# Decay and causal fill added by VectorE from rows spread over all partitions, and attention's order planned with seeds

## Chip, core and metric

One core of a Trainium2 chip runs the whole program in one launch. The metric is device time in microseconds of that core, the median of three runs. A profile of one further execution gives the trace.

## What is computed

Attention with a decay, then two feed-forward layers, all in float32. The core of it:

```python
q, k, v: (4, 8, 576, 64), f: (4, 8, 576)
scores = scale * np.matmul(q, k.transpose(0, 1, 3, 2))
cum = np.cumsum(np.log(np.clip(f, 0.0001, 1.0)), axis=-1)
decay = cum[:, :, :, None] - cum[:, :, None, :]
scores = np.where(causal, -1000000000.0, scores + decay)
scores = scores - np.max(scores, axis=-1, keepdims=True)
attn = np.exp(scores)
attn = attn / (np.sum(attn, axis=-1, keepdims=True) + 1e-09)
x = (attn @ v) as (2304 tokens, 512)
h = x @ w_in;  x = (h / (1 + np.exp(-h))) @ w_out      # 2048 hidden
out = ((x @ w_a) * (x @ w_b)) @ w_out2                 # 1536 hidden
```

## The kernel before

*Attention.* The 32 heads go through in 16 pairs; the two heads of a pair lie on partitions 0 to 63 and 64 to 127 of one tile. A head's 576 query rows are five blocks (`IB`): four of 128 rows and one of 64. Block 0 meets 128 key columns, block 1 256, block 2 384, block 3 512; the two 64-row blocks of a pair share one pass over 576 columns, in two halves of 288. `score` (L519 on) makes the scores of a pair in the groups (4,), (3,), (2,), (1, 0), each in two of the four PSUM banks of tag `s`. A float32 product is made of three products in float32r: q and k are split into hi and lo (`load_parts`, L501: ScalarE or VectorE casts hi, GpSimd subtracts for lo in four pieces, L516), and hi·hi, hi·lo and lo·hi are summed in PSUM. In pairs 1 to 15 a fourth product comes first: the tile `dt` in bfloat16 holds, per head, six rows with the cumulative sum split in three bfloat16 parts and constants, so that this product gives the decay (L564, step 0). These rows are made in `prepare` (L437 to L449) and go through the DRAM tensor `dec`. Pair 0 (`QK32`) is made in whole float32 instead, with two extra rows for the decay (L558); its rows of the sum are loaded straight from `cum` (L489).

*After the scores.* VectorE reads a block from PSUM, adds the causal mask tile `maskw` or `mask2`, scales by -1/8 and takes the row minimum in one instruction (L590, `tensor_tensor_reduce`); the first half of the 64-row blocks needs no mask and has `tensor_scalar` (L586). ScalarE takes the exponential and the row sum (L598). TensorE turns the probabilities (L640), ScalarE or VectorE copies them out of PSUM (L645, L646), TensorE multiplies with v (L684), VectorE divides by the row sums, which come spread over partitions through DRAM (L613 to L621, L693), and ScalarE and GpSimd split the result into hi and lo of `x`.

*Feed-forward.* Weights come as float64 words and are decoded to float32 hi and lo (`plan_decode`, `decode`), in 13 chunks of hidden units. Chunk 0 and the decoding of chunks 0, 1 and 2 are planned together with attention; the products of chunk 0 (L766 to L768) are the filler work there. Chunk 1's tiles lie in a pool of their own and are decoded (`decode1`) while attention runs. From chunk 1 on (L311 to L313) the order is written by hand.

*Order.* Up to the end of chunk 0 the order of all engines comes from `Plan.order` (L171): a list scheduler that has a price for each operation (`t_mm`, `t_dve`, `t_act`, `t_pool`, and for DMAs the bytes divided by 230), a priority, and tags that count buffers; it takes the operation that can start first, and among those within 30 ns the one of the lowest priority value. Each engine runs its operations in the order that comes out. `keep_warm` puts small idle products (L805) where the plan sees TensorE idle early on; `run_up` puts 66 of them at the start.

## Time and profile before

| | |
|---|---|
| median of 3 runs | 1037.66 us (1037.36 to 1039.34) |
| the profiled execution: time, span | 1037.98 us, 1036.1 us |
| TensorE (PE) busy | 1020.9 us, 99% of the span |
| weight loads (PEld) | 846.7 us, 82% |
| VectorE (DVE) | 656.1 us, 63% |
| ScalarE (ACT) | 444.5 us, 43% |
| GpSimd (POOL) | 334.5 us, 32% |
| moved by DMA | 62.35 MB, mean 60 GB/s |

Busy time of an engine is the union of its instructions. Products on TensorE overlap: one may start 0.2 us after another and both last 0.4 us, so what a product costs is the distance to the next start. The row of a line and tile names what is written and read: `s<-decay` is a score bank written from the decay tile. A wait is put down to the engine whose semaphore came last.

### The profile page before, as it was taken

Reading aid. Unit: us, or ns where it says so; the run is one execution under the profiler, and the core shown is the slowest. Engines: PE = TensorE matmul, PEld = TensorE weight load, DVE = VectorE, ACT = ScalarE, POOL = GpSimd, SP = SyncE. Lnnn points to the kernel's source line nnn. Section 1 sums busy time; section 2 is a strip of 40 time slices with the busy share of each in tenths; the row PEclk is TensorE's granted clock in tenths of the full one; section 3 lists DMA queues with packets and bytes.
Section 4 is the critical chain, followed back from the end, with each engine's and each line's share of the span. In section 5 each row is a group of like instructions: output and inputs, shape, how many; then the busy total and the mean of one; then the engine's idle time right before and its main releaser. Section 6 shows DMA issues by size and latency. Waiting matters only on the chain.

```text
span 1036.1 us, 16198 instructions
## 1 busy us (share of the span) xinstructions
PE 1020.9 (99%) x5813; PEld 846.7 (82%) x5813; DVE 656.1 (63%) x1539; ACT 444.5 (43%) x1080; POOL 334.5 (32%) x414
## 2 busy tenths in 40 slices
PE   8989999999999999999999999999999999999998
PEld 7667777798888888888888788888888888888887
DVE  7885566648976856857648976166375485473334
ACT  7888888855433324323324445332132231231111
POOL 5574444434412503304006853051150150240000
PEclk9999999999999999999999999999999999999999
DMA  5443333212210201201101222021021030020012
GB/s 165 151 135 111 101 100 105 63 63 71 72 52 21 81 23 31 82 11 44 39 1 41 61 60 83 1 72 52 1 82 41 2 95 27 21 61 1 10 72 102
DMA packets 34096, 62.35 MB, mean 60 GB/s; under 512 B 7004, under 2 KB 8684, under 8 KB 33984
## 3 DMA queue, kind: packets, MB, share of 16 engines
q1 hardware_dynamic: 33904, 60.87, 19.0%
q8 instruction: 46, 0.75, 0.3%
q10 hardware_dynamic: 112, 0.45, 0.2%
q14 instruction: 34, 0.28, 0.1%
HBM read 56.05 MB, written 5.23 MB: 59 GB/s over the span
## 4 chain that ended last, share of the span: by engine, by line
PE 83%; DVE 5%; ACT 2%; issue 1%; DMA 1%; POOL 1%; POOLq 0%; ACTq 0%; DVEq 0%; SPq 0%
PE ps L311 14%; PE ps L313 14%; PE ps L312 14%; PE po L312 10%; PE po L313 9%; PE po L311 9%; PE s L564 3%; PE pv L684 3%; PE t_y L640 1%; PE t_x L640 1%; DVE acc L365 1%; DMA d<-in_w 1%; DVE d L277 1%; PE po L766 1%; PE ps L766 1%
## 5 line engine op out<-in xcount | busy, mean ns | idle before, releaser
L311 PE MATMUL ps<-x,whi 128*128 128x512 f32 (+1 forms) x760 | 279.9, 368 | 0.4 <-DVE acc L365 0.4
L312 PE MATMUL ps<-x,whi 128*128 128x512 f32 (+1 forms) x760 | 279.7, 368 | 0.0
L313 PE MATMUL ps<-x,wlo 128*128 128x512 f32 (+1 forms) x760 | 279.6, 368 | 0.0
L281 POOL TENSOR_TENSOR d<-d,whi 128x256 f32<-128x256 f32 x116 | 98.2, 850 | 420.8 <-ACT whi L280 379.0
L312 PE MATMUL po<-glo,whi 128*128 128x512 f32 (+1 forms) x520 | 191.4, 368 | 0.6 <-DVE glo L344 0.6
L313 PE MATMUL po<-ghi,wlo 128*128 128x512 f32 (+1 forms) x520 | 191.1, 368 | 0.0
L311 PE MATMUL po<-ghi,whi 128*128 128x512 f32 (+1 forms) x520 | 189.7, 369 | 0.6 <-ACT ghi L343 0.6
L311 PEld LDWEIGHTS ps<-x,whi 128*128 128x128 f32 x760 | 143.3, 189 | 24.8 <-issue 0.8
L313 PEld LDWEIGHTS ps<-x,wlo 128*128 128x128 f32 x760 | 143.3, 189 | 23.9
L312 PEld LDWEIGHTS ps<-x,whi 128*128 128x128 f32 x760 | 143.3, 189 | 23.7
L343 ACT CAST ghi<-g 128x512 fp32r<-128x512 f32 (+1 forms) x130 | 74.8, 576 | 141.6 <-DVE g L342 94.6
L311 PEld LDWEIGHTS po<-ghi,whi 128*128 128x128 f32 x520 | 97.9, 189 | 17.7 <-ACT ghi L343 1.4
L312 PEld LDWEIGHTS po<-glo,whi 128*128 128x128 f32 x520 | 98.1, 189 | 17.2 <-DVE glo L344 0.9
L344 DVE TENSOR_TENSOR glo<-g,ghi 128x512 fp32r<-128x512 f32 (+1 forms) x130 | 89.1, 686 | 35.7 <-ACT ghi L343 35.3
L313 PEld LDWEIGHTS po<-ghi,wlo 128*128 128x128 f32 x520 | 98.0, 188 | 16.3
L342 DVE TENSOR_TENSOR g<-g,ps 128x512 f32<-128x512 f32 (+1 forms) x60 | 37.9, 631 | 115.4 <-PE ps L313 114.8
L282 POOL TENSOR_TENSOR wlo<-d,d 128x256 fp32r<-128x256 f32 x116 | 91.2, 790 | 36.1 <-DVE d L279 32.8
L273 ACT ACTIVATE d<-d 128x256 f32<-128x256 f32 x116 | 50.5, 435 | 121.0 <-DMA d<-in_w 98.9
L365 DVE SCALAR_TENSOR_TENSOR acc<-po,acc 128x512 f32<-128x512 f32 (+3 forms) x144 | 76.2, 549 | 24.9 <-PE po L313 24.7
L274 DVE TENSOR_SCALAR d<-d 128x256 uint32<-128x256 uint32 x116 | 44.6, 384 | 63.5 <-ACT d L273 62.7
L374 DVE TENSOR_TENSOR acc<-po,acc 128x512 f32<-128x512 f32 (+2 forms) x120 | 64.5, 553 | 25.6 <-PE po L313 25.0
L341 ACT COPY g<-ps 128x512 f32<-128x512 f32 (+1 forms) x60 | 32.4, 540 | 103.8 <-PE ps L313 103.8
(129 smaller groups left out, 1486.7 us busy)
## 6 DMA issues: line engine op xcount, KB each, us to landing
d<-in_w SPq DMA_DIRECT2D x124, 256.0 KB
qk<-in_qk SPq DMA_DIRECT2D x15, 608.0 KB
vt<-in_v SPq DMA_DIRECT2D x16, 320.0 KB
rb<-invs SPq DMA_DIRECT2D x32, 128.0 KB
out_t<-acc SPq DMA_DIRECT2D x12, 256.0 KB
d2ghi<-in_w SPq DMA_DIRECT2D x8, 256.0 KB
e<-in_w SPq DMA_DIRECT2D x4, 256.0 KB
out_t<-acc SPq DMA_DIRECT2D x4, 192.0 KB
```

The costliest lines, as they stand in the source:

```text
L273: nc.scalar.activation(m, high.bitcast(F32), AF.Copy, scale=2.0 ** -112)
L274: nc.vector.tensor_scalar(m.bitcast(U32), m.bitcast(U32), 3, None, ALU.logical_shift_left)
L281: nc.gpsimd.tensor_sub(m, val, hi.bitcast(F32))
L282: nc.gpsimd.tensor_add(lo, m, e)
L311: nc.tensor.matmul(ps, wh, mh, start=start, stop=False)
L312: nc.tensor.matmul(ps, wh, ml, start=False, stop=False)
L313: nc.tensor.matmul(ps, wl, mh, start=False, stop=stop)
L342: nc.vector.tensor_mul(g, g, project(c, 1, t, t0, n)[:, :n])
L343: nc.scalar.copy(ghi[:, t, :n], g)
L344: nc.vector.tensor_sub(glo[:, t, :n], g, ghi[:, t, :n].bitcast(F32))
L365: nc.vector.scalar_tensor_tensor(a, ps, 0.5, a, ALU.mult, ALU.add)
L374: nc.vector.tensor_add(a, ps, a)
```

## The change

- The bfloat16 decay product of pairs 1 to 15 goes, with its tile `dt`. A row's own decay term is constant along the row and drops out of the softmax, so only the negated sum of the key columns, `cn` = -8 cum, remains to be added. It is stored once as `dec` (32 x 576 float32), and each pair loads it with every partition reading the same row: `ws` (64 partitions per head, 576 columns, for the 64-row blocks) and `wd[p]` (128 partitions, 512 columns, one per head).
- VectorE's `tensor_tensor_reduce` adds `ws` or `wd[p]` where it added the mask. `tensor_scalar` remains in pair 0 alone.
- The causal fill is put into these tiles by GpSimd: `hide` writes MASKED above the diagonal of 128 columns of `wd[p]`, first those of block 3; once VectorE has read block 3, those of block 2, and so on. For `ws` the 64-column mask is added once.
- Pair 0 takes q and k from the packed tile, both heads in halves of the array, and gets its `cn` row by an fp32 product with a selection matrix `sel` (`pick`, L572 of the new kernel).
- Chunk 1's weight tiles take the slots of `qkh` and its decoding those of `wd` and `p`, so it follows the last pair (`plan_early`).
- `shake` adds random amounts, by 60 fixed seeds, to the priorities of some operations. Prices change: DMA bytes by 330 in place of 230, ScalarE 2% and GpSimd 10% dearer, VectorE's decode steps half as dear again. `RUN_UP` is 30 in place of 66.

```diff
+SHAKES = (
+    98418, 636944, 799308, 878264, 960778, 981929, 617613, 565829, 424101, 929226, 581331, 653776,
...
+def shake(ops, seed):
+
+    rng = Random(seed)
+    n, by = rng.choice((1, 2, 4, 8, 30, len(ops) // 4)), rng.choice((0.3, 1.0, 3.0))
+    for op in rng.sample(ops, n):
+        op.prio += rng.gauss(0, by)
...
-        self.add("DMA", size / 230, lambda: None, reads, writes, 0, 950)
+        self.add("DMA", size / 330, lambda: None, reads, writes, 0, 950)
...
-    return base + n / 1.2
+    return 1.02 * (base + n / 1.2)
 
 
 def t_pool(n):
-    return 133 + 2.135 * n
+    return 146 + 2.35 * n
...
-    dec = dram.tile([NH, 6, 2, S], BF16, name="dec")
+    dec = dram.tile([NH, S], F32, name="dec")
...
-    rows_sb = dp.tile([NH, 6, 2, S], BF16, name="rows")
+    cn = dp.tile([NH, S], F32, name="cn")
+    maskw = dp.tile([P, 512], F32, name="maskw")
+    sel = dp.tile([NH, 3, P], F32, name="sel")
...
-    RUN_UP, WARM = 66, 40000
-    rows_keys = [("rows", n) for n in range(2)]
+    RUN_UP, WARM = 30, 40000
...
+        plan.add("DVE", 300, lambda: nc.vector.tensor_scalar(cn, cum, -1 / SCALE, None, ALU.mult), ["cum"], [("rows", "cn")], -8)
+        plan.dma(480, 74000, lambda: nc.scalar.dma_start(dec, cn), [("rows", "cn")], ["dec"], pr, eng="ACT")
+        plan.add("POOL", 200, lambda: nc.gpsimd.memset(sel, 1.0), (), [("rows", "sel")], -9.8)
+        for n, base, steps, op in ((0, 0, 0, ALU.is_equal), (1, -1, 0, ALU.is_equal)):
+            plan.add("POOL", 244, lambda n=n, base=base, op=op: nc.gpsimd.affine_select(
+                sel[:, n], sel[:, n], pattern=[[0, P]], compare_op=op, fill=0.0, base=base, channel_multiplier=1),
+                (), [("rows", "sel")], -9.8)
...
-        for n in range(3):
-            src = cum if n == 0 else rest[n - 1]
-            plan.add("DVE", 450, lambda n=n, src=src: nc.vector.tensor_copy(rows_sb[:, n, 0], src), [("c", n), "cum"], [("rows", n)], -8)
-            if n < 2:
-                plan.add("DVE", 750, lambda n=n, src=src: nc.vector.tensor_sub(rest[n], src, rows_sb[:, n, 0]),
-                         [("c", n), ("rows", n), "cum"], [("c", n + 1), ("f", "one")[n]], -8)
-        for n in range(3):
-            plan.add("ACT", 530, lambda n=n: nc.scalar.copy(rows_sb[:, 3 + n, 1], rows_sb[:, n, 0]), [("rows", n)], [("rows", "k", n)], -8)
...
+    def hide(wd, n, pr):
+        plan.add("POOL", 300, lambda: nc.gpsimd.affine_select(
+            wd()[:, n * P:(n + 1) * P], wd()[:, n * P:(n + 1) * P], pattern=[[-1, P]], compare_op=ALU.is_ge,
+            fill=MASKED, base=0, channel_multiplier=1), (), [(wd, n)], pr + PRIO["max"])
...
+        wd = [buf(sb, "wd", [P, 512], F32, f"wd_{pair}_{p}") for p in range(2)]
+        ws = buf(sb, "ws", [P, S], F32, f"ws_{pair}")
...
+        def wide(h, rows, n):
+            src = dec[h]
+            return bass.AP(tensor=src.tensor, offset=src.offset, ap=[[0, rows], [1, n]])
+
         for p in range(2):
-            plan.dma(400, 0, lambda p=p: nc.sync.dma_start(
-                dt()[p * D:p * D + 6, :2 * S], dec[2 * pair + p].rearrange("r i t -> r (i t)")), ["dec", ("decay", n)], [(dt, p)], pr)
-            plan.dma(400, 0, lambda p=p: nc.sync.dma_start(
-                dt()[p * D:p * D + 6, 2 * S + p * D:2 * S + (p + 1) * D], dec[2 * pair + p, :, 0, 512:]), ["dec", ("decay", n)], [(dt, 2 + p)], pr)
+            plan.dma(480, 4 * D * S, lambda p=p: nc.sync.dma_start(ws()[p * D:(p + 1) * D], wide(2 * pair + p, D, S)),
+                     ["dec"], [(ws, p)], pr)
+        plan.add("POOL", 270, lambda: nc.gpsimd.tensor_add(ws()[:, -D:], ws()[:, -D:], mask2[:, -D:]),
+                 [(ws, 0), (ws, 1), ("const", 3)], [(ws, "m")], pr)
+        for p in range(2):
+            plan.dma(480, 4 * P * 512, lambda p=p: nc.sync.dma_start(wd[p](), wide(2 * pair + p, P, 512)),
+                     ["dec"], [(wd[p], n) for n in range(4)], pr)
+            hide(wd[p], 3, pr)
...
-                    a, b = ((t["dt"],) * 2, (t["hi"], t["hi"]), (t["hi"], t["lo"]), (t["lo"], t["hi"]))[step]
+                    out = banks[part]()[:, :nj] if shared else banks[p]()[:, at:at + nj]
+                    a, b = (t["s1"],) * 2 if whole else ((t["hi"], t["hi"]), (t["hi"], t["lo"]), (t["lo"], t["hi"]))[step]
                     a, b = (half(x(), p) if p is not None else x() for x in (a, b))
-                    k0, q2 = (2 * S - S, 2 * S) if step == 0 else (512, Q2)
-                    stat = a[:, i] if p is not None else a[:, q2:q2 + P]
-                    nc.tensor.matmul(out, stat, b[:, k0 + j0:k0 + j0 + nj], start=step == 0, stop=step == 3)
...
+            if whole:
+
+                def pick(at=at, nj=nj):
+                    for n in range(2):
+                        out, j0 = (banks[n]()[:, :nj], n * nj) if shared else (banks[n]()[:, at:at + nj], 0)
+                        nc.tensor.matmul(out, sel[:, 2 if shared else n], cn[:, j0:j0 + nj], start=False, stop=True)
+
+                plan.add("PE", 2 * (nj / 0.6 + 20), pick, [("rows", "cn"), ("rows", "sel")], banks, pr + PRIO["s"], mode=PICK)
...
+            t = heads[2 * pair]
+            if whole:
+                add, keys = (lambda p=p, nj=nj: (mask2 if p is None else maskw)[:, -nj:]), [("const", 3) if p is None else ("rows", "mask")]
+            elif shared:
+                add, keys = (lambda t=t, j0=j0, nj=nj: t["ws"]()[:, j0:j0 + nj]), [(t["ws"], n) for n in (0, 1, "m")]
             else:
-                mk = mask2[:, -nj:] if p is None else maskw[:, -nj:]
-                plan.add("DVE", t_dve(nj) + 82, lambda out=out, low=low, o=o, mk=mk: nc.vector.tensor_tensor_reduce(
-                    out(), o(), mk, -SCALE, 3.0e38, ALU.add, ALU.min, low()), [s, ("const", 3)], [(b, j0), (nm, col)], pr + PRIO["max"])
+                add, keys = (lambda t=t, p=p, nj=nj: t["wd"][p]()[:, :nj]), [(t["wd"][p], n) for n in range(ib + 1)]
+            plan.add("DVE", t_dve(nj) + 82, lambda out=out, low=low, o=o, add=add: nc.vector.tensor_tensor_reduce(
+                out(), o(), add(), -SCALE, 3.0e38, ALU.add, ALU.min, low()), [s, *keys], [(b, j0), (nm, col)], pr + PRIO["max"])
+            if not whole and not shared and ib:
+                hide(t["wd"][p], ib - 1, pr)
...
-        plan.add("DVE", t_dve(n, True), lambda: nc.vector.tensor_scalar(u(m), u(m), 3, None, ALU.logical_shift_left),
+        plan.add("DVE", 1.5 * t_dve(n, True), lambda: nc.vector.tensor_scalar(u(m), u(m), 3, None, ALU.logical_shift_left),
...
+    def plan_early(pr):
+        w1 = [buf(keep, "qkh", [P, chunks[1][4]], F32R, f"w{n}1") for n in ("hi", "lo")]
+        wtiles[1] = tuple((lambda w=w: w()) for w in w1)
+        for i in range(chunks[1][4] // W0):
+            tiles = [buf(sb, t, [P, W0 * k], F32, f"e{n}_{i}") for n, (t, k) in enumerate((("wd", 2), ("wd", 1), ("p", 1), ("p", 1)))]
+            plan_decode(1, i * W0, W0, tiles, w1, ("w1", i), pr + i)
...
+    for seed in SHAKES:
+        shake(plan.ops, seed)
```

What it moves. On TensorE, the 512-column scores of pair 3 (`s_3_3_0` and `s_3_3_1`, one bank per head), before:

```order
L564 LDWEIGHTS decay0_97
L564 MATMUL s_3_3_0_812<-decay0_97 128x512
L564 LDWEIGHTS decay0_97
L564 MATMUL s_3_3_1_814<-decay0_97 128x512
L564 MATMUL s_3_3_0_812<-qkh_3_687 128x512
L564 MATMUL s_3_3_1_814<-qkh_3_687 128x512
L564 MATMUL s_3_3_0_812<-qkl_3_712,qkh_3_687 128x512
L564 MATMUL s_3_3_1_814<-qkl_3_712,qkh_3_687 128x512
L564 MATMUL s_3_3_0_812<-qkh_3_687,qkl_3_712 128x512
L564 MATMUL s_3_3_1_814<-qkh_3_687,qkl_3_712 128x512
```

Four steps for the two heads, the decay first. And now:

```order
L557 MATMUL s_3_3_0_777<-qkh_3_546 128x512
L557 MATMUL s_3_3_1_779<-qkh_3_546 128x512
L557 MATMUL s_3_3_0_777<-qkl_3_569,qkh_3_546 128x512
L557 MATMUL s_3_3_1_779<-qkl_3_569,qkh_3_546 128x512
L557 MATMUL s_3_3_0_777<-qkh_3_546,qkl_3_569 128x512
L557 MATMUL s_3_3_1_779<-qkh_3_546,qkl_3_569 128x512
L557 MATMUL s_3_2_0_792<-qkh_3_546 128x384
```

The products with the decay tile are gone, and the three of hi and lo stand alone.

On VectorE, the score passes of pair 9, before (`nm` collects the row minima):

```order
L590 ISA p_9_0_3_2057,nm_9_1964<-s_9_3_0_1977,maskw_61 128x512
L590 ISA nm_9_1964 128x1
L590 ISA p_9_1_3_2068,nm_9_1964<-s_9_3_1_1979,maskw_61 128x512
L590 ISA nm_9_1964 128x1
L780 SCALAR_TENSOR_TENSOR g_1_288_2055<-g_1_288_2055,ps_1_288_1918 128x288
L590 ISA p_9_0_2_2082,nm_9_1964<-s_9_2_0_1997,maskw_61 128x384
L590 ISA nm_9_1964 128x1
```

All read one mask tile, `maskw`. On VectorE now, the same passes read `wd_9_0` and `wd_9_1`:

```order
L595 ISA p_9_0_3_2127,nm_9_2046<-s_9_3_0_2058,wd_9_0_1815 128x512
L595 ISA nm_9_2046 128x1
L595 ISA p_9_1_3_2138,nm_9_2046<-s_9_3_1_2060,wd_9_1_1826 128x512
L595 ISA nm_9_2046 128x1
L595 ISA p_9_0_2_2161,nm_9_2046<-s_9_2_0_2074,wd_9_0_1815 128x384
L595 ISA nm_9_2046 128x1
L595 ISA p_9_1_2_2172,nm_9_2046<-s_9_2_1_2076,wd_9_1_1826 128x384
L595 ISA nm_9_2046 128x1
L595 ISA p_9_0_1_2200,nm_9_2046<-s_9_1_0_2163,wd_9_0_1815 128x256
```

The operation and its order stay; its second input is now a tile that GpSimd changes between the passes. On GpSimd (POOL) now, the selects of pair 9's tiles, the residuals `qkl_11` and the other work between them:

```order
L510 TENSOR_TENSOR ws_11_2070<-ws_11_2070,mask2_61 128x64
L490 AFFINE_SELECT wd_9_0_1815<-wd_9_0_1815 128x128
L490 AFFINE_SELECT wd_9_1_1826<-wd_9_1_1826 128x128
L490 AFFINE_SELECT wd_9_0_1815<-wd_9_0_1815 128x128
L490 AFFINE_SELECT wd_9_1_1826<-wd_9_1_1826 128x128
L490 AFFINE_SELECT wd_9_0_1815<-wd_9_0_1815 128x128
L520 TENSOR_TENSOR qkl_11_2217<-qk_11_1858,qkh_11_2206 128x304
L490 AFFINE_SELECT wd_9_1_1826<-wd_9_1_1826 128x128
L520 TENSOR_TENSOR qkl_11_2217<-qk_11_1858,qkh_11_2206 128x304 x3
```

Each VectorE pass from the third on reads a tile whose select stands on GpSimd behind the pass before it; the residuals stand around the last select.

On TensorE at the start, pair 0's scores, before:

```order
L805 MATMUL idle_120<-maskb_60,identb_59 128x128
L558 MATMUL s_0_4_0_228<-whole0_102 64x288
L558 MATMUL s_0_4_0_228<-whole1_112 64x288
L558 MATMUL s_0_4_1_231<-whole0_102 64x288
L558 MATMUL s_0_4_1_231<-whole1_112 64x288
L558 MATMUL s_0_3_0_237<-whole0_102 128x512
L558 MATMUL s_0_3_1_239<-whole1_112 128x512
```

Each head's product is whole in one step. And now, with the products of `cn` and `sel` behind them:

```order
L816 MATMUL idle_116<-maskb_60,identb_59 128x128
L557 MATMUL s_0_4_0_164<-whole_104 128x288
L557 MATMUL s_0_4_1_166<-whole_104 128x288
L557 MATMUL s_0_3_0_170<-whole_104 128x512
L557 MATMUL s_0_3_1_172<-whole_104 128x512
L572 MATMUL s_0_4_0_164<-cn_73,sel_75 128x288
L572 MATMUL s_0_4_1_166<-cn_73,sel_75 128x288
L572 MATMUL s_0_3_0_170<-cn_73,sel_75 128x512
L572 MATMUL s_0_3_1_172<-cn_73,sel_75 128x512
L557 MATMUL s_0_2_0_195<-whole_104 128x384
L557 MATMUL s_0_2_1_197<-whole_104 128x384
L572 MATMUL s_0_2_0_195<-cn_73,sel_75 128x384
```

The first four banks are written twice before block 2 begins.

## Rows read from the trace of the kernel before

**Rows 1.** Busy time by stretch: length, then busy (instructions) of PE, PEld, DVE, ACT, POOL, PEclk, DMA share, GB/s.

```profile
30.00:75.00 45.00, 41.44 (x365) 29.13 (x363) 38.30 (x122) 38.06 (x105) 29.86 (x37) 1.00 0.47 148
...
100.00:200.00 100.00, 98.41 (x859) 74.18 (x857) 62.62 (x237) 84.51 (x244) 43.61 (x55) 1.00 0.31 97
...
600.00:700.00 100.00, 100.00 (x477) 84.25 (x476) 55.50 (x115) 41.92 (x97) 37.46 (x47) 1.00 0.17 51
```

**Rows 2.** Waits, 75 to 200 us: who waited for whom, total us, times, longest.

```profile
DVE p L590 <- PE t_x L640: 10.8, 8, 1.9
```

**Rows 3.** Timeline of PE, scores of pair 6 and 7: start, us, engine, line, tiles.

```profile
79.46 0.39 PE L564 MATMUL s<-decay 64*128 64x512 bf16 x2
...
80.39 0.34 PE L564 MATMUL s<-decay 64*128 64x384 bf16 x2
...
87.91 0.28 PE L564 MATMUL s<-decay 64*128 64x256 bf16 x2
...
88.38 0.23 PE L564 MATMUL s<-decay 64*128 64x128 bf16 x2
...
93.48 0.30 PE L564 MATMUL s<-decay 128*128 128x288 bf16 x1
...
94.01 0.30 PE L564 MATMUL s<-decay 128*128 128x288 bf16 x1
```

**Rows 4.** Groups of instructions: the decay products, busy us, mean ns.

```profile
L564 PE MATMUL s<-decay 128*128 128x288 bf16 (+4 forms) x150 | 28.0, 304 | 0.9 <-DVE nm L590 0.7 <-DVE p_None L586 0.2
```

**Rows 5.** Timeline of all engines, the first 20 us.

```profile
3.08 6.15 PE L420 MATMUL idle<-maskb,identb 128*128 128x128 bf16 x66 [3.08 <-DVE identb L414]
...
4.07 1.35 DVE L429 TENSOR_TENSOR_SCAN cum<-one,ft 32x576 f32<-32x576 f32 x1 [0.75 <-ACT ft L426]
...
6.71 0.58 SPq L506 DMA_DIRECT2D qk<-in_qk  x1
...
9.07 1.22 PE L805 MATMUL idle<-maskb,identb 128*128 128x128 bf16 x19
...
10.22 3.10 PE L558 MATMUL s<-whole 66*64 66x288 f32 x12
...
11.17 0.36 ACTq L448 DMA_DIRECT2D dec<-rows  x1
...
11.57 1.21 ACT L512 CAST qkh<-qk 128x1216 fp32r<-128x1216 f32 x1 [0.48 <-DMA qk<-in_qk]
...
11.88 0.19 PEld L558 LDWEIGHTS s<-whole 66*128 66x128 f32 x1 [0.24 <-issue]
...
12.31 0.19 PEld L558 LDWEIGHTS s<-whole 66*128 66x128 f32 x1 [0.24 <-issue]
...
12.91 3.20 POOL L516 TENSOR_TENSOR qkl<-qk,qkh 128x304 fp32r<-128x304 f32 x4 [2.15 <-ACT qkh L512]
...
14.90 0.33 SPq L508 DMA_DIRECT2D decay<-dec  x1
...
19.21 0.29 PE L564 MATMUL s<-decay 128*128 128x288 bf16 x1
```

**Rows 6.** Timeline: a select on POOL, a score pass, two decode passes, POOL's work then.

```profile
1.43 0.29 POOL L412 TENSOR_SCALAR_AFFINE_SELECT ident<-ident 128x128 f32<-128x128 f32 x1
...
13.36 0.69 DVE L590 CUSTOM_DVE_ANT_0 p<-s,maskw 128x512 f32<-128x512 f32 x1 [0.16 <-PE s L558]
...
26.36 1.83 POOL L516 TENSOR_TENSOR qkl<-qk,qkh 128x304 fp32r<-128x304 f32 x2
...
27.41 1.05 DVE L719 SCALAR_TENSOR_TENSOR d1g<-d2ghi,d1glo 128x256 uint32<-128x256 uint32 x1
...
61.18 0.42 DVE L719 SCALAR_TENSOR_TENSOR d1g<-d2ghi,d1glo 128x256 uint32<-128x256 uint32 x1
```

**Rows 7.** The page's DMA queues: packets, MB, share of 16 engines.

```profile
q1 hardware_dynamic: 33904, 60.87, 19.0%
```

**Rows 8.** Timeline of PE where chunk 1 begins; the row ahead is L311's first product.

```profile
240.75 0.39 PE L312 MATMUL ps<-x,whi 128*128 128x512 f32 x1
```

More of the change, by code (lines that the diff above doesn't have):

```diff
@@ L550, in mm @@
                     j0 = part * nj
-                    i = slice(i0, i0 + ni)
-                    if not shared:
-                        out = banks[p]()[:, at:at + nj]
-                    else:
-                        out = banks[part]()[slice(None) if p is None else slice(p * D, (p + 1) * D), :nj]
-                    if whole:
-                        a = t["s1"]().bitcast(F32)
-                        nc.tensor.matmul(out, a[:D + 2, 0, i], a[:D + 2, 1, j0:j0 + nj], start=True, stop=True)
-                        return
@@ L564, in mm @@
[L564 removed]
+                    stat = a[:, i0:i0 + ni] if p is not None else a[:, Q2:Q2 + P]
+                    nc.tensor.matmul(out, stat, b[:, 512 + j0:512 + j0 + nj], start=step in (0, 3), stop=step == 2)
                 t = heads[2 * pair + (p or 0)]
                 mms.append(mm)
[L568 to L571 removed]
+                keys.append((t["s1"], "h"))
@@ L572, in score @@
+                if not whole:
+                    keys += [(t["lo"], "l", c0) for c0 in range(0, QK, QK // 4)]
             keys = list(dict.fromkeys(keys))
-            dur = 2 * (nj / 0.6 + 20) if whole else 8 * t_mm(nj) if shared else 4 * t_mm(nj)
-            plan.add("PE", dur, lambda mms=mms: [mm() for mm in mms], keys, banks, pr + PRIO["s"],
-                     mode=(COLUMNS if shared else WHOLE) if whole else WHOLE if shared else ROWS)
+            dur = (2 if shared else 1) * (nj / 0.6 + 20 if whole else 3 * t_mm(nj))
@@ L827, in model_kernel @@
         if pair == NH // 2 - 1:
-            for i in range(chunks[1][4] // W0):
-                decode1(i, heads[2 * pair]["s1"], 1000 + i)
+            plan_early(1000)
         if pair % 4 == 3:
```

99 lines of the change are left out of this document (34 added, 65 removed), and 4 rows, old and new, of the table SHAKES.

## The prediction

> **What bounds the kernel now.** I read first the busy time by stretch, because the program has two parts: sixteen pairs of heads of attention with the first weight chunk mixed in, then twelve more chunks of feed-forward work. In the second part TensorE is busy for the whole of a 100 us stretch, and VectorE, ScalarE and GpSimd are at 56, 42 and 37% [rows 1]. That part begins at about 240.5 us [rows 8], the change leaves its products alone, so it costs the same and only begins earlier or later. Everything is decided before 240.5 us.
>
> There the stretches differ. From 100 to 200 us TensorE is busy 98.4 of 100 us, ScalarE 84.5, VectorE 62.6, GpSimd 43.6. From 30 to 75 us TensorE has 41.4 of 45, and VectorE and ScalarE have 38 each, 85%: nobody has much room [rows 1]. The view of waits, taken from 75 to 200 us, says who paces whom: VectorE's score passes wait for TensorE, 10.8 us in eight times [rows 2]. So from 75 us on TensorE's work is the time, nearly one to one, and before that it is one of three limits.
>
> **The change part by part.** *Decay products.* Each score has four steps on TensorE: the bfloat16 decay product and three products of the split q and k. The change drops the first. Its records overlap their neighbours, so their durations, 28.0 us in all [rows 4], are not the price; the price is the distance between starts [rows 3]. The 512-column score begins at 79.46 and the next at 80.39: four steps in 0.93, 0.23 each. The 256-column one takes 87.91 to 88.38, 0.12 a step; 384 lies between, 0.17; 128 I put at 0.10, under the 0.12. A 288-column half takes 93.48 to 94.01, 0.13 a step, and there are two. Per pair 0.23 + 0.17 + 0.12 + 0.10 + 0.27 = 0.89 us; 150 products are 30 of each of five forms, two heads or halves in each of 15 pairs [rows 4], so 13.4 us of TensorE's time goes. If the work follows TensorE alone it is all gained; if it follows another engine, nothing. The score at 79.46 is pair 6's. Pairs 6 to 15 are ten: **8.9 us**, which I take whole, because feed-forward products of the first chunk stand there to fill gaps. Pairs 1 to 5 have no such filler until batch 0 is complete, and two other engines at 85%: 0 to 4.5, I take half, **2.2 us**.
>
> *The start.* The first score product waits for rows of the cumulative sum that two queues load into its operand: the sum ends at 5.42 (4.07 + 1.35) and the product starts at 10.22 [rows 5]. Now the scores of pair 0 need only the q,k tile, whose load is issued near 1.3 us; a load of that size issued at 6.71 was there at 11.57, 4.9 us later [rows 5], so about 6.3. That is 3.9 us earlier. Against it, the row of the sum is now added by fp32 products of a selection matrix. Two halves of a 512-column fp32 product, which runs as two, start at 11.88 and 12.31 [rows 5], so 512 columns cost 0.86; the added products cover 2 x 1280 + 576 columns, 5.3 us. The two heads' own products now run side by side in halves of the array, which saves one head's 1280 columns, 2.1 us. Net 3.0 to 3.2 us more. Also, though the granted clock is 1.00, the 2.4 GHz level, in the stretches shown [rows 1], TensorE's first 66 products take 6.15 us, 93 ns each, and the 19 behind them 64 ns [rows 5]; the run-up shrinks from 66 to 30, so some slow time, 0.5 us, falls on real work. Pair 0 ends hardly sooner (3.9 - 3.1 - 0.5 = 0.3).
>
> Pair 1 gains more. Its decay rows went through a store to DRAM issued at 11.17 and loads issued from 14.90, and its first product ran at 19.21 [rows 5]. The store now needs one VectorE pass after the sum, so about 6.0, and the loads of the spread rows can go at about 9.7. GpSimd's order puts a select on the first of them ahead of the q,k residuals. Those four took 3.20 us from 12.91, once the cast that had its input at 11.57 was done [rows 5]; with selects and an addition between them (three at about 0.3) and rows that land by about 13, I get 17.3: **1.8 us** earlier, with 0 (the rows come as late as the old ones) and 3 (they cost no wait) as ends.
>
> *The addition.* VectorE reads each score once, scales it and takes the row minimum, and already adds a tile from SBUF to every part but one half per pair. It now adds the spread rows instead of the mask: 0.69 us for 512 columns [rows 6], the same operation, so nothing. The one half changes from a scaling pass to this operation of the same size, 15 of them, at most 0.1 us each, in VectorE's idle 37 of 100 us.
>
> *The causal fill.* It is 120 selects of 128x128 on GpSimd, eight per pair, nearest row 0.29 us for that shape [rows 6], and 15 small additions at 0.35, an estimate between that and the 0.80 of a 304-column one [rows 5]: 40 us of GpSimd, 2.7 us per pair in its idle 56 of 100 [rows 1]. Three times per pair and head VectorE must wait for a select that itself waits for VectorE's previous pass. The other head's pass (0.69, later 0.55 and 0.42) stands between and covers 0.29 plus the hand-over, if GpSimd is free. Behind the select on GpSimd stand the residuals of the next pair, behind the waiting pass on VectorE the exponentials' inputs and score banks. I cost it at nothing, with the case where the cover is gone below.
>
> What VectorE may lose is the shared access to SBUF. A decode step with two inputs in SBUF takes 0.42 us alone and 1.05 where GpSimd works beside it; the score pass, with one input in PSUM, takes 0.69 with GpSimd at work beside it too [rows 5, 6]. So the decode steps feel the new GpSimd time and the score passes don't; for the casts of q,k, which also stay within SBUF, the rows leave it open. The Trainium skill, page SBUF — State Buffer, section Who interferes with whom, calls this a lock held for a whole instruction, taken by a VectorE instruction with two SBUF inputs or in its two-port modes; the rows agree for decode steps (0.42 to 1.05), and no row here shows a cast that waits. What that would make of the time is rival C.
>
> *Loads.* Per pair 0.82 MB of repeated rows replace 28 KB, by the tiles' sizes. The whole queue moved 60.87 MB in 19.0% of sixteen engines' 1036.1 us [rows 7], 309 GB/s when moving, so 2.6 us of a pair's 12 (eight pairs in 100 us), 21%, on the 31% of 100 to 200 us and the 47% of 30 to 75 us [rows 1]. It fits, and the loads are issued a pair ahead. The number of issues per pair stays at 11 on SP's queue. Nothing.
>
> *The second weight chunk.* Its four decode steps move from the middle to behind the last pair, into tiles that attention frees. There VectorE and GpSimd have room and first-chunk products cover it; I take 0.5 us as lost.
>
> *Order by seeds.* The planner now shuffles its priorities, and its costs are set anew. From 30 to 75 us TensorE idles 3.6 us and from 100 to 200 us 1.6 [rows 1]. How much of it another order closes, or whether it opens more, the trace cannot say: the ends are a gain of 5.2 and a loss of as much; I take a gain of 2.5, because the filler products in the built order fall from 99 to 60.
>
> **The sum:** 8.9 + 2.2 + 1.8 + 2.5 - 0.5 = 14.9 (pair 0's 0.3 is contained in pair 1's 1.8). The profiled execution took 1037.98 (span 1036.1): 1023.1. The median of the runs, 1037.66, is 0.3 below it, so **1022.8 us**.
>
> **The rivals.** *A, the forecast,* chance 0.52, by itself 1018 to 1028. For it: TensorE at 98% and others waiting for it.
>
> *B, the new order closes nearly all gaps* and pairs 1 to 5 follow TensorE too: 14.9 + 2.7 + 2.3 = 19.9, **1017.8**. For it: the filler products again. Against: VectorE and ScalarE at 85% before 75 us. Chance 0.17.
>
> *C, another engine paces attention.* GpSimd's new work stretches casts and decode steps: 15 casts that each wait for one GpSimd operation, 0.8 [rows 5], are 12 us; the 16 two-input decode passes of chunk 0 could lose 0.63 each [rows 6], but some already do, so 3 more; ScalarE would stand at 84.5 of 92.9, 91%, once the eight pairs in those 100 us lose their 0.89. If half of those 15 reach TensorE, 7.5 of the gain goes: **1030.3**. Chance 0.19, no more because VectorE's idle 37 of 100 us [rows 1] lies in the way. The Trainium skill's rule just named is this case.
>
> *D, the freed time turns into waits* for repeated rows or selects, pair by pair 0.9: **about 1037**, chance 0.05.
>
> *E, slower.* VectorE's in-order wait for selects becomes the bound: at each of three levels a pair the select stands behind one 304-column residual, 0.80 [rows 5], with no cover, 2.4 us per pair against 0.89 saved. Over 15 pairs that is 22 us lost; with some 10 us of first-chunk products to fill them, **about 1050**. It decides from 0.9 us of uncovered wait per pair on. Against: the order sets residuals mostly behind the selects. Chance 0.07.
>
> **How the numbers follow.** This kernel's runs tell apart about 0.2%, 2.1 us. A, B and C are faster: 0.88. D is the same: 0.05. E is slower: 0.07. The range runs from 1015, a little below B, to 1032, a little above C, which also takes in the bounds of the start (0 to 3), of pairs 1 to 5 (0 to 4.5) and of the order; it leaves out D, E and the tails of B and C, together under 0.2.
>
> **What would show it.** Second part unchanged in length, beginning near 226 instead of 240.5 us; the 512-column scores 0.70 apart; pair 1's first score near 17 us; VectorE's score passes unchanged in length, with waits for GpSimd's selects under 0.3 us per pair; TensorE at 98% from 75 us. Long waits of score passes for selects would speak for E, ScalarE above 90% with TensorE under 97% for C. A start of the second part later than 240 us would make the prediction wrong.

## The result, and the profile after

The changed kernel takes 1044.18 us (median of 4 runs, 1043.69 to 1045.60) against 1038.29 for the kernel before on the same chip: a ratio of 1.0056, 95% interval 1.0044 to 1.0068. It is slower by 0.6%, where 1022.8 was forecast. The profiled execution took 1044.42 (span 1042.7), so 21.3 us more than the sum's 1023.1.

Busy time by stretch, with the columns of [rows 1]:

```profile
8.00:30.00 22.00, 22.00 (x129) 14.81 (x126) 12.38 (x47) 11.32 (x34) 9.84 (x20) 0.77 0.72 196
30.00:75.00 45.00, 39.51 (x309) 27.23 (x307) 38.70 (x124) 36.97 (x111) 39.05 (x66) 0.96 0.66 204
100.00:200.00 100.00, 93.24 (x747) 71.64 (x747) 56.86 (x229) 80.33 (x234) 60.74 (x121) 0.97 0.53 153
600.00:700.00 100.00, 100.00 (x488) 84.72 (x487) 57.26 (x115) 41.92 (x97) 37.89 (x46) 1.00 0.17 48
```

Three things differ from [rows 1]. TensorE idles more: 5.5 of 45 us (before 3.6) and 6.8 of 100 (before 1.6). Its granted clock is no longer 1.00: 0.77, 0.96 and 0.97 are 10.1, 3.6 and 6.0 us at the 1.2 GHz level. And the DMA engines' share rose from 47 to 66% and from 31 to 53%. The second part is as it was. It begins later, though: its first product, forecast near 226, starts at 244.37, and some 3 us of the first chunk stand behind that.

```profile
244.37 0.39 PE L329 MATMUL ps<-x,whi 128*128 128x512 f32 x1
```

The view of waits from 30 to 200 us (engine, what waits, for what; us in all, times, longest) names what is new:

```profile
POOL wd L490 <- DMA wd<-dec: 17.2, 14, 3.3
DVE p L595 <- POOL wd L490: 15.2, 18, 2.7
ACT x L703 <- DVE xf L700: 12.3, 9, 3.0
DVE xf L700 <- DMA rb<-invs: 8.7, 7, 2.7
PEld t_x L647 <- DVE xf L700: 8.2, 8, 2.1
```

GpSimd's selects (L490) wait for the repeated rows `wd`, VectorE's score passes (L595) for the selects, and VectorE's output step (L700) for the reciprocals `rb`, which come through DRAM and are loads that the change did not touch. One instance, in the timeline of all engines:

```profile
158.45 1.26 SPq L626 DMA_DIRECT2D rb<-invs  x1
159.81 0.54 SPq L513 DMA_DIRECT2D wd<-dec  x1
160.45 0.44 SPq L508 DMA_DIRECT2D ws<-dec  x1
...
162.69 0.82 DVE L700 TENSOR_TENSOR xf<-pv,rb 128x448 f32<-128x448 f32 x2 [2.66 <-DMA rb<-invs]
...
163.78 0.37 PE L618 MATMUL rs<-ident,sm 128*9 128x128 f32 x1 [2.44 <-DVE sm L614]
...
164.11 0.29 POOL L490 TENSOR_SCALAR_AFFINE_SELECT wd<-wd 128x128 f32<-128x128 f32 x1 [3.31 <-DMA wd<-dec]
```

The selects' loads, issued from 159.81, stand behind the loads of `rb`, and those were late themselves. The store that they wait for was issued at 152.12 into a burst of loads (the DMA engines' share is 0.92 from 152 to 154 us), and the first load of `rb` followed 4.43 us later:

```profile
149.85 1.09 SPq L508 DMA_DIRECT2D ws<-dec  x2
151.36 0.34 SPq L501 DMA_DIRECT2D qk<-in_qk  x1
152.12 0.29 SPq L620 DMA_DIRECT2D invs<-rt  x1
156.55 0.45 SPq L628 DMA_DIRECT2D rb<-invs  x1
```

Between 30 and 200 us the median of this distance, from the issue of the store to that of the first load, is 3.05 us; before it was 2.05.

In the instance VectorE stands 2.66 us for reciprocals; the next pair's sum is behind that on VectorE, so TensorE stands 2.44; GpSimd stands 3.31 for rows with the residuals of x behind it. At 163.5 the granted clock falls.

At the start TensorE is busy all the time and yet late:

```profile
8.66 2.95 PE L572 MATMUL s<-cn,sel 32*128 32x288 f32 x8
11.54 0.92 PE L557 MATMUL s<-whole 64*128 64x384 f32 x4
12.39 2.03 PE L572 MATMUL s<-cn,sel 32*128 32x384 f32 x4
...
15.50 2.07 PE L572 MATMUL s<-cn,sel 32*128 32x256 f32 x4
...
22.38 0.59 PE L557 MATMUL s<-qkh 128*128 128x288 f32 x1
```

From 13.3 to 23.6 us the clock is at 1.2 GHz: the selection products' 256 columns take 2.07, as long as the 384 that began before the fall. Pair 1's first score comes at 22.38; it was 19.21 [rows 5], and 17.3 was forecast.

The DMA view, against [rows 7]: 12 MB more.

```profile
q1 hardware_dynamic: 39824, 72.75, 23.4%
wd<-dec SPq DMA_DIRECT2D x30, 256.0 KB
ws<-dec SPq DMA_DIRECT2D x30, 144.0 KB
```

### The profile page after: what moved, and what is told of

Read it like the earlier page. It is cut to its first block, busy times and chain, and to the rows that moved or that the text cites. A ratio compares the mean times of both kernels' runs of the same rounds, so it can differ in the third digit from the quotient of the medians.

```text
span 1042.7 us, 16041 instructions
## 1 busy us (share of the span) xinstructions
PE 1021.5 (98%) x5604; PEld 847.3 (81%) x5604; DVE 654.7 (63%) x1534; ACT 437.5 (42%) x1076; POOL 371.1 (36%) x548
## 4 chain that ended last, share of the span: by engine, by line
PE 74%; DVE 3%; issue 1%; DMA 0%; ACT 0%; POOL 0%; SPq 0%; DVEq 0%; POOLq 0%
PE ps L329 14%; PE ps L330 14%; PE ps L331 14%; PE po L330 10%; PE po L329 10%; PE po L331 10%; DVE acc L383 1%; DVE d L295 1%; DMA d<-in_w 0%; DVE d L297 0%; DVE glo L362 0%; DVE d L293 0%; PE po L778 0%; PE po L779 0%; PE po L777 0%
## 5 line engine op out<-in xcount | busy, mean ns | idle before, releaser
L329 PEld LDWEIGHTS po<-ghi,whi 128*128 128x128 f32 x520 | 97.9, 189 | 17.7 <-POOL d L734 0.8
L330 PEld LDWEIGHTS po<-glo,whi 128*128 128x128 f32 x520 | 98.0, 189 | 17.3 <-DVE glo L362 0.9
L362 DVE TENSOR_TENSOR glo<-g,ghi 128x512 fp32r<-128x512 f32 (+1 forms) x130 | 88.3, 679 | 34.6 <-ACT ghi L361 34.3
L298 ACT CAST whi<-d 128x256 fp32r<-128x256 f32 x116 | 46.0, 405 | 72.6 <-DVE d L293 60.7
```

The source lines that it names most:

```text
L298: nc.scalar.copy(hi, val)
L329: nc.tensor.matmul(ps, wh, mh, start=start, stop=False)
L330: nc.tensor.matmul(ps, wh, ml, start=False, stop=False)
L362: nc.vector.tensor_sub(glo[:, t, :n], g, ghi[:, t, :n].bitcast(F32))
```

## The experiments

The theories: the loads are late (T), the selects (S), the order (O), the clock at the start (R: the few rows of its products). Each time is a median; ratios are to the kernel before on the same chip. Its median was 1037.8 to 1038.6 from chip to chip, so a difference between two runs can be off by most of a microsecond.

**Rows loaded once**, into tiles kept for even and odd pairs (`ws` likewise):

```diff
-            plan.dma(480, 4 * P * 512, lambda p=p: nc.sync.dma_start(wd[p](), wide(2 * pair + p, P, 512)),
+            plan.dma(480, 4 * P * 512, lambda p=p: nc.sync.dma_start(wd[p](), wide(2 * pair + p, P, 512)) if pair < 3 else None,
```

> The changed kernel whose repeated rows are loaded for pairs 1 and 2 alone; the other 13 pairs add those two pairs' rows again, so their decay is another pair's. Every instruction of TensorE, VectorE, ScalarE and GpSimd, the selects too, stays in its place; 41 loads, about 9.6 MB, are gone from SP's queue. Theory T, late transfers: between 30 and 200 us GpSimd waits 17.2 us in 14 selects for these loads and VectorE 15.2 us in 18 score passes for selects, and the loads of the reciprocals come late beside them (VectorE waits 8.7 us in 7). If that is what keeps TensorE idle, its idle time from 30 to 200 us falls from 14.2 us to 8 or less, the granted clock no longer falls after 24 us (6.8 us regained there), and the time is 1030 to 1036 us. Theory S, the selects themselves are what VectorE waits for: the waits of score passes stay above 10 us and the time is 1041 to 1045. Theory O, the seeded order itself makes the gaps: idle time stays at 13 or more and the time is 1043 to 1045.

1029.57 us, 0.9916 (0.9901 to 0.9930): T, by 14.6 us. (The loads left out are in fact 52, of 10.6 MB.) From the store of the reciprocals to the first load of them the median is now 1.37 us.

```profile
30.00:75.00 45.00, 41.09 (x323) 28.33 (x320) 40.56 (x128) 37.85 (x112) 41.98 (x70) 0.96 0.47 150
100.00:200.00 100.00, 99.88 (x835) 77.94 (x835) 62.81 (x245) 89.30 (x264) 64.36 (x126) 1.00 0.30 91
```

With every select in place TensorE has 99.88 of 100 us. The waits, in the same stretch as above:

```profile
DVE p L595 <- POOL wd L490: 7.5, 12, 1.3
...
DVE xf L700 <- DMA rb<-invs: 0.2, 1, 0.2
```

**No selects**:

```diff
-        plan.add("POOL", 300, lambda: nc.gpsimd.affine_select(
...
+        plan.add("POOL", 300, lambda: None,
```

> The changed kernel without the 120 selects on GpSimd: the causal fill of pairs 1 to 15 is left out, everything else is issued as before, the 60 loads of repeated rows too. Theory S: GpSimd's 40 us of selects and the hand-over to VectorE and back are the cost; without them the waits of score passes fall to those for loads, idle time of TensorE from 30 to 200 us falls to 8 or less and the time to 1030 to 1036 us. Theory T: the loads are as late as before, VectorE now waits for them itself, and GpSimd is no longer held up by them; a part of the gain only, 1036 to 1042. Theory O: 1043 to 1045.

1040.31, 1.0029 (1.0017 to 1.0041): 3.9 us, theory T's range. VectorE waits 16.7 us in ten for reciprocals there (8.7 after): the loads are still late, only found elsewhere.

**128 rows in the selection products**:

```diff
-    cn = dp.tile([NH, S], F32, name="cn")
+    cn = dp.tile([P, S], F32, name="cn")
...
-    sel = dp.tile([NH, 3, P], F32, name="sel")
+    sel = dp.tile([P, 3, P], F32, name="sel")
...
+        plan.add("DVE", 607, lambda: [nc.vector.memset(one, 1.0), nc.vector.memset(cn, 0.0)], (), ["one"], pr)
...
```

> The changed kernel with the selection matrix and the negated sum of pair 0 widened from 32 to 128 partitions, with zeros in the new ones: the same products over the same columns, four times the rows; one more VectorE fill of 128x576 at the start. Theory R, the granted clock falls at 13.3 us because TensorE runs products of 32 rows there: with 128 rows it stays at 2.4 GHz from 8 to 30 us, pair 1's first score comes at 17 to 18 instead of 22.4, and the time falls by 3 to 5 us, to 1039 to 1041. Theory F, it falls with fp32 products of this kind whatever their rows: the clock falls near 13 us again, pair 1's first score stays near 22.4, and the time is 1043 to 1045.

1042.79, 1.0044 (1.0030 to 1.0058). The clock stays at 2.4 GHz until 22.7, and pair 1 comes 4.6 us earlier:

```profile
12.16 1.56 PE L572 MATMUL s<-cn,sel 128*128 128x384 f32 x4
...
17.83 0.38 PE L557 MATMUL s<-qkh 128*128 128x288 f32 x1
...
22.85 0.48 PE L647 MATMUL t_x<-ident,p_None 128*128 128x128 f32 x1 [2.28 <-ACT th L652]
```

R holds for the clock at 13 us, but at most 1.4 us reach the end (the intervals with and without overlap): TensorE then waits 2.28 us for a copy by ScalarE, and from 22.7 the clock is at 1.2 GHz for 3.4 us.

**More products** behind each product call of pair 0 (`dead(n)` issues n bfloat16 products into the idle bank):

```diff
-                        nc.tensor.matmul(out, sel[:, 2 if shared else n], cn[:, j0:j0 + nj], start=False, stop=True)
+                        nc.tensor.matmul(out, sel[:, 2 if shared else n], cn[:, j0:j0 + nj], start=False, stop=True); dead(2)
```

> The changed kernel with two bfloat16 128x128 products into the idle bank behind each of pair 0's 20 product calls, 40 in all, which at 2.4 GHz add about 2.5 us. Theory A, the granted clock falls at 13.3 us because TensorE does too little for it there, and more products hold it: it stays at 2.4 GHz from 8 to 30 us, pair 0's products end 2 to 3 us earlier than at 19.4 in spite of the added ones, and the time is 1040 to 1043. Theory F, the clock falls for another reason or these are too few: it falls near 13 us again, pair 1's first score comes 2 to 5 us later than at 22.4, and the time is 1045 to 1049.

1057.99, 1.0190 (1.0175 to 1.0205), far over every expectation: the clock is at 1.2 GHz from 14.4 to 38.2.

```profile
8.39 1.12 PE L557 MATMUL s<-whole 64*128 64x512 f32 x2
9.44 0.28 PE L396 MATMUL idle<-maskb,identb 128*128 128x128 bf16 x2
9.66 1.12 PE L557 MATMUL s<-whole 64*128 64x512 f32 x2
```

The added products part the two heads' halves, which now run one behind the other, still at the higher level here: 1.12 us for each 512 columns, where both heads' 384 took 0.92 together. So the run does not test what it was made for.

**More buffers**, six and three in place of four and two, in the same order:

```diff
+    REAL = dict(wd=6, ws=3)
...
-        n = SLOTS[tag]
+        n = REAL.get(tag, SLOTS[tag])
```

> The changed kernel with six buffers in place of four for a head's repeated rows and three in place of two for the shared block's; the order on every engine and queue is that of the change. Without the loads the time was 1029.6 us, so they cost about 14.6. Theory B, they are late because a buffer comes free late: SP's queue waits 11.5 us in ten loads of one kind and 12.3 in nine of the other for VectorE's last pass over the old rows (30 to 200 us). With more buffers these waits go, GpSimd's selects wait under 6 us for loads instead of 17.2, and half or more of the 14.6 comes back: 1032 to 1038. Theory Q, they cost because 0.82 MB per pair stands ahead of the small store and load of the reciprocals in one queue: started earlier they are as long, VectorE still waits 8 us or more for reciprocals, and the time is 1040 to 1045.

1040.80, 1.0018 (1.0007 to 1.0030): 3.4 us, a quarter of the 14.6. SP's queue no longer waits for buffers, and the selects still wait 16.6 us in 14 for loads: theory B is not the main cost.

And these loads on **ScalarE's queue** besides (`ws` likewise):

```diff
-            plan.dma(480, 4 * P * 512, lambda p=p: nc.sync.dma_start(wd[p](), wide(2 * pair + p, P, 512)),
+            plan.dma(480, 4 * P * 512, lambda p=p: nc.scalar.dma_start(wd[p](), wide(2 * pair + p, P, 512)),
```

> As the kernel with six and three buffers, and the loads of repeated rows are issued on ScalarE's queue instead of SP's, at the same place of the order. Theory Q: the store and the load of the reciprocals no longer stand behind 0.82 MB, SP's waits for the store (22.5 us in eight and 16.1 in five) fall below 20 together, VectorE waits under 4 us for reciprocals, and the time is 1030 to 1036. Theory B: no further gain over the kernel with more buffers alone, within 2 us of it. Theory W, the bytes themselves hold the sixteen engines whichever queue they come from: reciprocals stay late, within 2 us of the kernel with more buffers, or slower, since ScalarE now waits for buffers in its own order.

1043.99, 1.0053 (1.0035 to 1.0070): slower again, as W allows. The Trainium skill (page DMA: Bandwidth & Descriptors, section Queues, rings and completion order) says that a DMA engine takes turns between queues, packet by packet; by that the small store should have slipped past the rows. From the issue of the store of the reciprocals to that of the first load of them, which waits for it, the median is 2.47 us here, 2.88 with more buffers alone, 3.05 after and 2.05 before: a little of it, and no gain in time.

**Traffic alone, in the kernel before**, beside the loads of its decay rows (`junk` is in DRAM):

```diff
+        load = lambda to, rows, n: nc.sync.dma_start(to[:rows * n].rearrange("(r n) -> r n", n=n), bass.AP(tensor=qk.tensor, offset=qk[pair].offset, ap=[[0, rows], [1, n]]))
...
+            plan.dma(400, 0, lambda p=p: [nc.sync.dma_start(
+                dt()[p * D:p * D + 6, :2 * S], dec[2 * pair + p].rearrange("r i t -> r (i t)")), load(junk[pair, 1024 * P + p * D * S:], D, S)], ["dec", ("decay", n)], [(dt, p)], pr)
...
```

> The kernel before with four more transfers per pair of the change's sizes, 0.82 MB of a repeated row into DRAM that nothing reads, issued beside the loads of the decay rows on SP's queue; nothing waits for them. What their traffic alone costs, without selects and without a reader: theory Q or W, the reciprocals come late here too, VectorE's waits for them rise from 2.7 us to 8 or more between 30 and 200 us and the time by 5 to 12 us, to 1043 to 1050. Theory B, the cost is in the waits of the rows' own readers: within 2 us of the kernel before, 1037 to 1040.

1081.74, 1.0429 (1.0404 to 1.0453), far over the range: transfers that nobody reads cost 44 us, and VectorE's waits for reciprocals grow from 2.7 us in two to 26.0 in six:

```profile
DVE xf L693 <- DMA rb<-invs: 26.0, 6, 6.6
```

They stand right ahead of the loads of `rb` on SP's queue and write DRAM, so the size is not the change's own. What carries over is that unread bytes on this queue make the reciprocals late.

**No seeds**:

```diff
-    for seed in SHAKES:
+    for seed in ():
```

> The changed kernel with no seeds: priorities stay as they are written, everything else, the new costs too, as in the change. The prediction counted 2.5 us for the seeds with ends of 5.2 either way. If they give what it said, 1046 to 1048; if the order that they make is itself what opens the gaps, 1036 to 1042; if the seeds have been drawn for this kernel and carry more than that, over 1050.

1047.49, 1.0087 (1.0064 to 1.0110): the seeds give 3.3 us where 2.5 was counted, with intervals that overlap. The clock does not fall here until 45 us, with the same 32-row products (8.79 where the changed kernel has 8.66), and pair 1 begins at 18.43. So the seeded order loses at the start and wins more behind it; the new prices were not undone.

**Rows loaded once, and 128 rows**, both edits as above.

> Both cures together: repeated rows loaded for pairs 1 and 2 alone (the other pairs add those rows again) and the selection matrix over 128 partitions. If late rows and the clock at the start are all that the prediction missed, the time comes near its 1022.8: with rows loaded once it is 1029.6, and the 128 rows bring pair 1's first score from 22.4 to 17.8 us, 4.6 earlier, which nothing now takes back: 1024 to 1026, with the first chunk's end 4 us sooner. If something else in the start takes it back, as it did with all the loads in place (only 1.4 of 4.6 were left), 1028 to 1030.

1028.46, 0.9905 (0.9891 to 0.9920): the second expectation. Pair 1 starts at 17.7, pair 2 at 34.3 where it was 33.7, since ScalarE stands at the head of its queue for the first weights, issued at 13.63 behind the rows of the first pairs:

```profile
22.69 0.43 ACT L722 ACTIVATE d1glo<-d2ghi 128x256 f32<-128x256 f32 x1 [3.81 <-DMA d2ghi<-in_w]
```

**Only the shared block's rows loaded once**:

```diff
-            plan.dma(480, 4 * D * S, lambda p=p: nc.sync.dma_start(ws()[p * D:(p + 1) * D], wide(2 * pair + p, D, S)),
+            plan.dma(480, 4 * D * S, lambda p=p: nc.sync.dma_start(ws()[p * D:(p + 1) * D], wide(2 * pair + p, D, S)) if pair < 3 else None,
```

> Only the shared block's rows are loaded for pairs 1 and 2 alone (26 loads of 144 KB, 3.8 of the 10.6 MB that were taken away before; the last block of the other pairs adds those two pairs' rows); the loads for which selects wait stay. Theory W, the cost goes with the bytes on the sixteen engines: 36% of 14.6 us come back, 1037 to 1041. Theory P, it is GpSimd's wait for the larger loads at the head of its queue: nothing comes back, 1042 to 1045.

1031.97, 0.9941 (0.9926 to 0.9956), below both ranges: 36% of the bytes give 12.2 of 14.6 us.

```profile
100.00:200.00 100.00, 98.30 (x816) 75.60 (x815) 60.36 (x241) 87.58 (x259) 62.80 (x124) 1.00 0.41 128
```

**128 rows with more buffers**, then **with a planner that knows of them** (`wd=6, ws=3` in `SLOTS`).

> The selection matrix over 128 partitions, with six and three buffers for the repeated rows; all of the computation is kept. Apart they gave 1.4 and 3.4 us. If they add up, 1038 to 1040, about the kernel before. If the late rows decide the pace from pair 2 on whatever the start does, 1040 to 1042.

1038.82, 1.0004 (0.9991 to 1.0016): they add up, to the time before.

> The same, but the planner too knows of six and three buffers and sets the loads, and with them the whole order, by that. If loads that are issued a pair sooner are on time: selects wait under 6 us for them between 30 and 200 us, and the time is 1033 to 1037, under the kernel before. Theory W: the bytes hold the engines whenever they are issued, 1039 to 1043.

1056.05, 1.0162 (1.0134 to 1.0189), a miss: the whole order changes, pair 2 starts at 37.7, and why it is so much worse was not followed up.

**The same bytes, unread**:

```diff
+            plan.dma(480, 4 * D * S, lambda p=p: nc.sync.dma_start((ws() if pair < 3 else kept("unread", [P, S]))[p * D:(p + 1) * D], wide(2 * pair + p, D, S)),
```

> The shared block's rows loaded for pairs 1 and 2 alone, and for the other pairs loads of the same bytes from the same places on the same queue into a tile that nobody reads; the last block of those pairs adds the rows of pairs 1 and 2. Without these loads it was 1032.0 us, with them and their readers 1044.2. Theory W, the bytes: reciprocals and the other rows are late again, 1040 to 1045. Theory P, what waits for them (GpSimd's addition waits 7.7 us in six between 30 and 200 us, with selects and residuals behind it): 1031 to 1035.

1039.62, 1.0024 (1.0014 to 1.0034; runs from 1038.9 to 1044.0), just under W's range: W for the most part. 7.7 of the 12.2 us come with the bytes alone, and the waits grow (9.5, 10.8 and 2.7 without these loads):

```profile
POOL wd L490 <- DMA wd<-dec: 14.0, 15, 1.9
DVE p L595 <- POOL wd L490: 12.6, 17, 3.0
...
DVE xf L700 <- DMA rb<-invs: 7.0, 5, 2.9
```

**The small addition on VectorE**, ahead of the pass that reads it, alone and with the two cures:

```diff
-        plan.add("POOL", 270, lambda: nc.gpsimd.tensor_add(ws()[:, -D:], ws()[:, -D:], mask2[:, -D:]),
+        plan.add("POOL", 270, lambda: None,
...
+ ... nc.vector.tensor_add(ws()[:, -D:], ws()[:, -D:], mask2[:, -D:]) ...
```

> The changed kernel with the small addition of the causal fill to the shared block's rows on VectorE, just ahead of the pass that reads it, in place of GpSimd; all loads and all of the computation are kept. Theory P: GpSimd's queue is no longer held for these rows, 1034 to 1039, at a price of 15 additions of some 0.15 us on VectorE. Theory W: 1042 to 1046.

1044.24, 1.0059 (1.0042 to 1.0076): nothing, so GpSimd's wait for that addition is not what the other 4.5 us are.

> The addition on VectorE, the selection matrix over 128 partitions, and six and three buffers for the repeated rows; all of the computation is kept. The last two alone gave 1038.8. Theory P: 1030 to 1035, clearly under the kernel before. Theory W: 1037 to 1040.

1040.25, 1.0017 (1.0004 to 1.0031): nothing again.

**Fewer bytes, whole computation**: no `ws` loads; both heads' rows of the shared block come from one bfloat16 product, and the last part adds the plain mask.

```diff
+                    by = shared and not whole
+                    if by and step == 0:
+                        nc.tensor.matmul(out, rowsel[:, 2 * pair:2 * pair + 2].rearrange("r h c -> r (h c)"), cn3[:, j0:j0 + nj], start=True, stop=False)
...
+            if shared and not whole:
+                add = lambda nj=nj: mask2[:, -nj:]
```

`cn3` holds the scaled sum in three bfloat16 parts on 96 partitions, `rowsel` ones where a row's head is.

> The changed kernel without the shared block's repeated rows (30 loads of 144 KB): its decay is added on TensorE again, by one bfloat16 product per half that selects both heads' rows from the sum split in three, 30 products of 288 columns at 0.13 us, 4 us in all; with the selection matrix over 128 partitions and six buffers for the rows that stay; all of the computation is kept. Theory W: what the loads cost, 12.2 us, comes back, less 4 for the products and plus 1 for the start: 1044.2 - 12.2 + 4 - 1 gives 1035, range 1032 to 1037, under the kernel before. If the products fall into the pairs' gaps and cost less: 1031 to 1033. If the extra work at the start (a copy of 2048 columns on ScalarE, five small steps on VectorE) delays pair 1, or the larger loads alone fill the queue: 1038 to 1042.

**1026.55**, 0.9887 (0.9870 to 0.9903): faster than both kernels, and below every range. Part of that is the start: pair 2 begins at 29.25, where rows loaded once with 128 rows had 34.3. Why the whole is over 4 us below the lowest range was not followed up.

```profile
8.00:30.00 22.00, 22.00 (x174) 14.75 (x173) 16.52 (x61) 17.47 (x51) 12.62 (x21) 1.00 0.67 214
30.00:75.00 45.00, 41.44 (x323) 30.13 (x322) 38.91 (x125) 37.03 (x108) 40.52 (x68) 0.96 0.56 178
100.00:200.00 100.00, 99.25 (x836) 77.96 (x832) 59.86 (x231) 86.90 (x255) 61.94 (x116) 1.00 0.42 130
```

The second part begins at 226.29, the forecast's place, but with some 4 us of the first chunk behind it. In the timeline the next start is 0.03 us behind the added product (L573):

```profile
18.26 0.29 PE L573 MATMUL s<-cn,rowsel 96*128 96x288 bf16 x1
18.29 0.39 PE L574 MATMUL s<-qkh 128*128 128x288 f32 x1
18.52 0.29 PE L574 MATMUL s<-qkl,qkh 128*128 128x288 f32 x1
```

That is not its price: from start to start over 100 to 185 us, a pair's two halves of 288 columns take 1.08 us with it and 0.91 without (rows loaded once), so 0.17 a pair and 2.6 us in all.

**That kernel with one part undone**: four buffers, then 32 rows.

> The kernel that gave 1026.6 us (shared block's decay by products, selection matrix over 128 partitions, six buffers for the rows that stay) with four buffers again; all of the computation is kept. If the buffers matter only where the loads are late, within 1 us: 1026 to 1028. If the late buffers were a cost of their own, as the 3.4 us in the changed kernel suggest: 1029 to 1031.

1027.03, 0.9896 (0.9881 to 0.9911): the buffers are worth nothing that shows.

> The kernel that gave 1026.6 us with the selection matrix of 32 partitions again; all of the computation is kept. The granted clock falls to 1.2 GHz near 13 us for about 10 us again, and pair 1's first score comes near 22 us instead of 18.3. If that shift of the start reaches the end: 1029 to 1031. If what follows is bound by the first weights' loads and the pairs before batch 0 is whole, as with rows loaded once (1029.6 and 1028.5): 1026.5 to 1028.5.

1030.80, 0.9930 (0.9914 to 0.9947): the clock at the start is worth about 4.2 us once the loads leave room. Even so this kernel is under the kernel before.

## Why the prediction was wrong

**Loads, "Nothing": this step failed.** The prediction set 21% of the queue's time a pair beside a mean share of 31 to 47% and found room. A mean hides order: a pair's rows, q,k and v go out in one burst, and the 4.5 KB store of reciprocals and the loads that wait for it come late (3.05 us from one to the other, 2.05 before, 1.37 with rows loaded once). "Issued a pair ahead" did not help either: the first reader of a row is a select on GpSimd, which stood 3.31 us for one. Rows loaded once gave back 14.6 us; bytes that nobody reads cost 7.7 for the smaller kind alone. The other 4.5 us of that kind stay open: GpSimd's addition is not it, and whether the 3.4 us that more buffers gave belong to it, no run separates. Why a third of the bytes costs most of the time is open too. Another place for the loads on SP's queue, and the planner's old price for DMAs (230), were not tried.

**Decay products: mis-sized.** A score was split into four equal steps of 0.23. But without the decay the 512-column score still takes 0.80 where [rows 3] have 0.93. Two lines of the kernel before, between those of [rows 3], then the changed kernel:

```profile
79.50 0.59 PE L564 MATMUL s<-qkh 64*128 64x512 f32 x2
79.93 0.39 PE L564 MATMUL s<-qkl,qkh 64*128 64x512 f32 x2
...
109.99 0.50 PE L557 MATMUL s<-qkh 64*128 64x512 f32 x2
110.32 0.39 PE L557 MATMUL s<-qkl,qkh 64*128 64x512 f32 x2
110.56 0.40 PE L557 MATMUL s<-qkh,qkl 64*128 64x512 f32 x2
110.79 0.33 PE L557 MATMUL s<-qkh 64*128 64x384 f32 x2
```

The steps are not equal. Before, the first two took 0.47 together (0.04 and 0.43); now hi·hi alone takes 0.33, so 0.14 goes and not 0.23. Summed from start to start over all scores from 100 to 185 us, a pair takes 3.25 us with rows loaded once and 3.81 before: 0.56 saved, not 0.89; 8.4 us over 15 pairs, not 13.4. The sum took 11.1 of the 13.4, pairs 1 to 5 at half; by the same count 0.56 gives 7.0.

**The start: failed.** "0.5 us of slow time" was 10.2 us at the lower level, while TensorE was busy. What was forecast without it (17.3) is what 128 rows give (17.8 and 18.3). The term of 1.8 became a loss; curing it is worth 4.2.

Loads 14.6, products 4.1 (11.1 less 7.0) and the start 4.2 make 22.9, where 21.3 were missed. Each was measured with other things changed, so the agreement proves little.

**The addition and the second part: held.** The 512-column pass takes 0.68 against 0.69 [rows 6]; the last stretch is unchanged.

**Order by seeds: not contradicted, and no more.** 3.3 us for 2.5, but the intervals overlap, the loads are late in both kernels, and the run without seeds kept its clock at the start. That the number came out near is in part luck.

**Causal fill: its mechanism came, its cause was another.** 15.2 us of waits are over the 0.9 us a pair from which rival E decides. But the selects waited above all for loads (17.2 us), and with the loads gone 7.5 us of the score passes' waits were left, at no cost: TensorE was at 99.88%. Rival D named the waits for rows and gave them 0.05; the loss went past its 1037. Rival C did not come: in the changed kernel ScalarE stands at 80% where C wants 90, and with rows loaded once it stands at 89 and GpSimd at 64% with TensorE full. One cast of q,k took 1.48 us beside GpSimd (median 0.79), at no cost that shows. The Trainium skill (page SBUF — State Buffer, section Who interferes with whom), from which the prediction has that rival's rule, counts casts among what can wait there; this one fits that, the median does not show it.

**What carries over.** Before costing a transfer at nothing, follow what is issued behind it and who waits for that: a small store and the loads that wait for it are delayed by the burst, not by the mean share. Price a removed product by the distance with and without it, not by an equal part of its group. Where a change makes one engine's operand out of memory traffic, move only as much as hides: here the blocks of 128 rows on VectorE and the shared one on TensorE beat both kernels, with the clock at the start cured (1026.55) and without (1030.80).

## What the runs showed of the hardware

The granted clock fell at 13.3 us in a stretch where TensorE was busy 22.00 of 22.00 us (8 to 30). With selection products of 32 rows it fell near 13 us in ten profiles of eleven, the exception being the run without seeds; with 128 rows, over the same columns, in none of seven before 22 us. So a busy TensorE alone did not keep the clock; why the run without seeds kept it, these runs don't settle. Later falls came behind idle time: in the changed kernel 1.30 us at 136.0 ahead of the fall at 139.6, and 2.44 us from 161.3, at whose end it fell (163.5). A gap of 1.3 us was not always followed by one: with only the shared block's rows loaded once, the gap at 70.0 was not.

In the changed kernel two heads' products of 384 columns, in halves of the array, took 0.92 us together. In the run with two full-size products between the heads, each head's 512 columns took 1.12 us, one behind the other.
